# Banded attention and a mixture layer in one kernel: another order for the first fourteen steps

## The chip, the cores and the metric

The kernel runs on one core of a Trainium2 chip. The metric is the device time of one execution in microseconds (us). The engines are PE (matrix products), DVE (element-wise and reductions), ACT (activations, copies), POOL (another element-wise engine) and SP, which here only issues loads and stores.

## The reference

```python
k_sum = k.reshape(B, H, nb, block, D).max(axis=3)
v_sum = v.reshape(B, H, nb, block, D).mean(axis=3)
mask_l = np.abs(pos[:, None] - pos[None, :]) < window
scores_s = scale * np.einsum('bhsd,bhnd->bhsn', q, k_sum) + np.log(block)
scores_all = np.concatenate([np.where(mask_l, scores_l, -1e9), scores_s], axis=-1)
a = softmax(scores_all)          # over window keys and block keys together
x = (a @ np.concatenate([v, v_sum], axis=2)) as tokens x 512
h = x @ w_in
P = a[0] + a[1] * h + a[2] * h**2 + a[3] * h**3
Q = 1.0 + np.abs(b[0]) * np.abs(h) + np.abs(b[1]) * h**2
out = (P / (Q + 1e-06)) @ w_out
```

(shortened; the lines of the softmax are drawn together.) There are B = 4 images, H = 8 heads, S = 768 positions, D = 64, block 32 and window 16; 3072 tokens go through w_in (512 x 2048) and w_out (2048 x 512).

## The kernel before

**Tiles.** A *half* is 64 query positions of all eight heads: 12 per image, 48 in all. A half needs 96 window keys and the 24 block keys, so its scores are a 128 x 480 tile. Eight halves are the 512 tokens of one *group*, of which there are six. The 2048 hidden units are cut into 16 *chunks* of 128. A *step* is one group with one chunk: 12 matmuls of layer 1 (`moe1`), the rational activation (the "gelu" of the names), 12 matmuls of layer 2 (`second_layer`).

**A half** (`half`) goes: scores on PE (`sc`), mask and minimum on DVE (`ss`, `sm`), exponentials and sums on ACT, reciprocal of the sum on DVE, normalization on POOL or DVE, transpose on PE (`pt`), copy of it on DVE or ACT (`pts`), product with the value rows on PE (`av`), then the sum as a rounded part `xh` (ACT or DVE) and a rest `xl` (DVE). The first eight halves are the inputs of group 0; halves 8 to 15 follow between the steps.

**The value rows** of a half are 96 loaded rows (`vw0`, `vw1`, `vr0` to `vr3` and two in `vlast`) and, below them, the 24 block means. These means are made once for image 0 by 10 products on PE (`vf`), copied twice by ACT (into `vw0` and `vw1`) and from there six times by POOL (`first_means`).

**The weights** of a chunk come in one load of 1 MB (`w_load`, tile `wr`) as 64-bit numbers and are turned on the chip into a high part and a low part: ACT scales the upper words (`Prelu`), POOL takes a byte of the lower words, DVE shifts and joins the two, ACT rounds the high part into `wearly`, and DVE subtracts for the low part (`w_split`, one token for each). There are four buffers for these loads; a chunk's buffer comes free when its low part is done.

**The order.** Up to step 13 a string, `TEXT`, says in what order all this is issued. Each token is a letter and a number: `K` and `k` load and reduce the keys of image 0 (`I` and `i` of image 1), `Q` loads queries, `V` value rows of a half, `A` windows of later halves, `F` and `G` value tiles, `S` sets constants, `W` loads a weight chunk, `w` does the next part of its split, `h` the next part of a half, `v` a product for the value means, `m` the copies of the means, `x` a third of layer 1 of a step, `ga` to `gk` a part of its activation, `y` a quarter of layer 2, `u` and `n` the means of image 1. The class `Kept` chains the instructions of each engine, and SP's loads, in the order of the text:

```python
if self.last is not None:
    tc.add_manual_dep(ins, self.last, ORDERED, reason="order of the text")
if self in strict:
    self.last = ins.name
```

So within an engine nothing passes anything else; between engines only semaphores count. Behind the text a loop runs over the remaining steps, with only PE in a fixed order.

Of the kernel before, what the change touches and what calls it, by code (L numbers as in the profile page):

```python
# [44 lines left out]
LAG = 3  # L45
SOFF = 12
NWARM = 6
TEXT = ("K2 K1 K0 Q0 K3 Q1 k2 k0 V2 V0 F0 V5 V1 k1 S0 k3 h0 h1 W0 V6 h0 V4 V3 h0 h1 h0 V7 W1 A8 h1 A9 h2 h3 h0 h2 h4 h3 v2 h1 h2 h3 h2 h4 v9 h0 h0 v0 h3 h1 h6 h2 v1 w0 h3 h2 W2 h3 "
# [11 lines left out]
AVGW = NK + NB - 4  # L60
AVGH = NK + NB - 2
NREST = (S - HPG * HQ) // P
# [22 lines left out]
def tile_kernel(ctx, tc, qw_in, kraw, kwin, vpad, vred, wio, a, b, cmask, cident, cavg, out):  # L85
# [635 lines left out]
    strict |= {pe, dve, act, gps, syn}  # L721
    for what in TEXT.split():
        token(what.rstrip("0123456789"), int(what.lstrip("abcdefghijklmnopqrstuvwxyzABCDEFGHIJKLMNOPQRSTUVWXYZ")))
# [99 lines left out]
```

## Time and profile before

| | |
|---|---|
| median of 3 runs | 637.9 us (636.54 to 637.99) |
| span of the profiled execution | 636.9 us |
| PE busy in that span | 620.4 us, 97% |
| DVE busy | 568.5 us, 89% |
| ACT busy | 457.1 us, 72% |
| POOL busy | 256.9 us, 40% |

The page gives no other time of the profiled execution than its span, the time from its first to its last instruction. Busy shares are means over the whole span; the text covers only the first 146 us or so, and there the engines stand in another relation to each other.

### The profile page before, as it was taken

The page shows a single profiled execution, that of the slowest core. Times are in us where ns is not written, and L with a number is a line of the kernel's source. Part 1 is how long each engine was busy: PE and PEld are TensorE (multiplying, and loading weights), DVE is VectorE, ACT ScalarE, POOL GpSimd, SP SyncE. Part 2 cuts the span into 40 slices and gives each one's busy share as a digit, 9 for nine tenths or more (in the row PEclk, how much of TensorE's full clock was granted, in tenths as well). Part 3 has the DMA queues.
Part 4 walks back from the last instruction along what each step waited for, and adds up shares of the span by engine and source line. Part 5 has one row for each costly group of instructions (what it writes and reads, how often), then busy time and mean ns, then how long its engine had stood idle before and what let it go on. Part 6 is the DMA issues. An engine that isn't in the chain of part 4 may idle for free.

```text
span 636.9 us, 11880 instructions
## 1 busy us (share of the span) xinstructions
PE 620.4 (97%) x4078; PEld 494.2 (78%) x4078; DVE 568.5 (89%) x1155; ACT 457.1 (72%) x1020; POOL 256.9 (40%) x344
## 2 busy tenths in 40 slices
PE   8899999999999999999999999999999999999997
PEld 4466777778788878888888777888888888888886
DVE  5799999999898999889988989988988989898885
ACT  3789999877867757767767768667777765656662
POOL 1366679654434336233143244243234242222221
PEclk9999999999999999999999999999999999999999
DMA  9977777413434434324423433323333120100001
GB/s 289 341 281 233 242 220 232 165 40 126 148 113 136 138 114 155 106 99 138 134 89 120 136 124 101 95 72 106 93 132 100 57 65 1 63 4 1 1 2 66
DMA packets 51752, 77.66 MB, mean 122 GB/s; under 512 B 6260, under 2 KB 33524, under 8 KB 49772
## 3 DMA queue, kind: packets, MB, share of 16 engines
q1 hardware_dynamic: 50412, 74.75, 36.2%
q0 software_dynamic: 560, 1.77, 1.4%
q8 instruction: 32, 0.52, 0.3%
q10 hardware_dynamic: 720, 0.38, 0.2%
q14 instruction: 28, 0.23, 0.1%
HBM read 60.33 MB, written 14.73 MB: 118 GB/s over the span
## 4 chain that ended last, share of the span: by engine, by line
PE 62%; DVE 21%; ACT 6%; DMA 5%; issue 3%; POOL 2%; DVEq 0%; POOLq 0%; ACTq 0%
PE po L113 29%; PE h L113 28%; DVE tu L113 6%; DVE tq L113 5%; PE av L113 3%; DVE gh L113 2%; PE sc L113 2%; DMA wr<-in_wio_dram 2%; DVE wr L113 2%; ACT ta L113 2%; DMA kres<-in_kraw_dram 1%; DVE ss L113 1%; POOL ss L113 1%; DMA w<-wr 1%; ACT ss L113 1%
## 5 line engine op out<-in xcount | busy, mean ns | idle before, releaser
L113 POOL TENSOR_TENSOR gl<-tu,ta 128x512 fp32r<-128x512 f32 x96 | 129.4, 1348 | 296.5 <-DVE tu L113 140.3
L113 ACT ACTIVATE ta<-tq,cs 128x512 f32<-128x512 f32 x96 | 69.8, 727 | 80.5 <-DVE tq L113 79.6
L113 PE MATMUL po<-wearly,gh 128*128 128x512 f32 x384 | 120.3, 394 | 0.7 <-ACT o L113 0.7
L113 PE MATMUL po<-w,gh 128*128 128x512 f32 x384 | 119.7, 393 | 0.0
L113 POOL TENSOR_SCALAR ss<-ss,sm 128x120 f32<-128x120 f32 x176 | 84.3, 497 | 41.6 <-DVE sm L113 40.7
L113 PE MATMUL h<-xh,wearly 128*128 128x512 f32 x384 | 97.8, 394 | 1.6 <-DVE tu L113 1.0
L113 PE MATMUL h<-xh,w 128*128 128x512 f32 x384 | 96.8, 391 | 1.4 <-DVE sm L113 0.9
L113 PEld LDWEIGHTS h<-xh,wearly 128*128 128x128 f32 x384 | 71.5, 188 | 18.2 <-ACT ta L113 1.0
L113 PEld LDWEIGHTS po<-wearly,gh 128*128 128x128 f32 x384 | 70.8, 188 | 18.0 <-ACT o L113 2.4
L113 PEld LDWEIGHTS h<-xh,w 128*128 128x128 f32 x384 | 71.5, 188 | 17.0 <-ACT ta L113 1.3
L113 DVE SCALAR_TENSOR_TENSOR gh<-tu,cs,ta 128x512 fp32r<-128x512 f32 x96 | 73.8, 768 | 10.9 <-ACT ta L113 1.4
L113 PEld LDWEIGHTS po<-w,gh 128*128 128x128 f32 x384 | 71.2, 188 | 15.7 <-issue 1.1
L113 ACT ACTIVATE ss<-ss,sm 128x120 f32<-128x120 f32 x188 | 71.7, 385 | 12.2 <-DVE sm L113 12.2
L113 ACT ACTIVATE tu<-h,cs 128x512 f32<-128x512 f32 x96 | 74.7, 778 | 0.5 <-PE h L113 0.5
L113 PE MATMUL po<-w,gl 128*128 128x512 f32 x192 | 74.9, 390 | 0.0
L113 PE MATMUL po<-wearly,gl 128*128 128x512 f32 x192 | 74.8, 390 | 0.0
L113 DVE SCALAR_TENSOR_TENSOR tu<-tu,cs,tq 128x512 f32<-128x512 f32 x96 | 72.2, 753 | 2.6
L113 DVE SCALAR_TENSOR_TENSOR tu<-tu,cs,h 128x512 f32<-128x512 f32 x96 | 71.1, 741 | 2.2
L113 DVE SCALAR_TENSOR_TENSOR tq<-tq,gh 128x512 f32<-128x512 f32 x96 | 66.6, 694 | 2.7
L113 ACT ACTIVATE ta<-h,cs 128x512 f32<-128x512 f32 x95 | 64.6, 680 | 4.8 <-POOL gl L113 4.8
L113 DVE TENSOR_TENSOR tu<-tu,h 128x512 f32<-128x512 f32 x96 | 64.9, 676 | 0.1
L113 ACT ACTIVATE ta<-ta 128x512 f32<-128x512 f32 x96 | 60.8, 633 | 2.7
(92 smaller groups left out, 917.3 us busy)
## 6 DMA issues: line engine op xcount, KB each, us to landing
wr<-in_wio_dram SPq DMA_DIRECT2D x15, 1024.0 KB
cross<-tb SPq DMA_DIRECT2D x32, 256.0 KB
vw<-in_vpad_dram SPq DMA_DIRECT2D x42, 192.0 KB
kw<-in_kwin_dram SPq DMA_DIRECT2D x40, 192.0 KB
pts<-cross SPq DMA_DIRECT2D x96, 64.0 KB
out_dram<-o SPq DMA_DIRECT2D x23, 256.0 KB
qw<-in_qw_dram SPq DMA_DIRECT2D x40, 128.0 KB
kr<-in_kraw_dram SPq DMA_DIRECT2D x12, 384.0 KB
```

The costliest lines, as they stand in the source:

```text
L113: out = getattr(self.engine, name)(*args, **kw)
```

## The change

Only `TEXT` is replaced. Both lists have the same 566 tokens, and so the same instructions; the first line of each:

```diff
-TEXT = ("K2 K1 K0 Q0 K3 Q1 k2 k0 V2 V0 F0 V5 V1 k1 S0 k3 h0 h1 W0 V6 h0 V4 V3 h0 h1 h0 V7 W1 A8 h1 A9 h2 h3 h0 h2 h4 h3 v2 h1 h2 h3 h2 h4 v9 h0 h0 v0 h3 h1 h6 h2 v1 w0 h3 h2 W2 h3 "
...
+TEXT = ("K2 K0 k0 k2 K1 k1 K3 k3 h8 Q0 h0 Q1 S0 h0 h2 V2 h14 h0 h0 h4 F0 v2 h3 h11 h1 h1 h1 h6 v8 h3 h3 h3 h0 W0 h0 h1 h5 h5 h3 h3 h3 V3 h1 h1 v9 h1 h2 h6 V0 v0 V4 v4 h7 h7 h2 h5 h5 "
...
```

In the words of the kernel: the load of chunk 0 (`W0`) stands behind one half's value rows and ahead of the seven others, where it stood behind four; the scaling of chunk 0 (the first `w0`) stands behind the exponentials of six halves, where it stood behind those of four; the halves come in another order; and more of the splits of chunks 2, 3 and 4 stand ahead of the third part of layer 1 of step 0.

**SP, the first loads.** Here are SP's loads from the first value rows on, in the kernel before (`vr`, `vw` and `vlast` are value rows, `vf0` the value tile, `wr0` chunk 0; `in_cavg` are constants for the means). Ahead of them stand four loads of keys and two of queries in both kernels.

```order
L113 DMA vr0_115<-in_vpad_dram 96x512
L113 DMA vw0_103<-in_vpad_dram 96x512
L113 DMA kres_107<-in_cavg_dram 128x282
L113 DMA vf0_0_141<-in_vpad_dram 128x2x512
L113 DMA vr3_118<-in_vpad_dram 96x512
L113 DMA vw1_104<-in_vpad_dram 96x512
L113 DMA wr0_188<-in_wio_dram 128x2048
L113 DMA vlast_119<-in_vpad_dram 96x512
L113 DMA vr2_117<-in_vpad_dram 96x512
L113 DMA vr1_116<-in_vpad_dram 96x512
```

And after:

```order
L113 DMA vr0_115<-in_vpad_dram 96x512
L113 DMA kres_107<-in_cavg_dram 128x282
L113 DMA vf0_0_264<-in_vpad_dram 128x2x512
L113 DMA wr0_322<-in_wio_dram 128x2048
L113 DMA vr1_116<-in_vpad_dram 96x512
L113 DMA vw0_103<-in_vpad_dram 96x512
L113 DMA vr2_117<-in_vpad_dram 96x512
L113 DMA vlast_119<-in_vpad_dram 96x512
L113 DMA vw1_104<-in_vpad_dram 96x512
L113 DMA vr3_118<-in_vpad_dram 96x512
L113 DMA vlast_119<-in_vpad_dram 96x512
```

With the six loads ahead of these rows, chunk 0 was the thirteenth load and is the tenth; seven value-row loads now stand behind it, where four did.

**ACT, the scaling of chunk 0.** The rows of ACT around that scaling, `ACTIVATE wr0`, before; `ACTIVATE ss` x4 are the exponentials of a half, `ACTIVATE sm` finishes its sums:

```order
L113 ACTIVATE ss2_253,sm2_254<-ss2_253,sm2_254 128x120 x4
L113 ACTIVATE sm2_254<-sm2_254 128x4
L113 ACTIVATE ss3_293,sm3_294<-ss3_293,sm3_294 128x120 x4
L113 ACTIVATE sm3_294<-sm3_294 128x4
L113 ACTIVATE wr0_188<-wr0_188 128x1024
L113 ACTIVATE ss4_307,sm4_308<-ss4_307,sm4_308 128x120 x4
L113 ACTIVATE sm4_308<-sm4_308 128x4
L113 ACTIVATE ss5_383,sm5_384<-ss5_383,sm5_384 128x120 x4
L113 ACTIVATE sm5_384<-sm5_384 128x4
```

And after:

```order
L113 ACTIVATE ss5_329,sm5_330<-ss5_329,sm5_330 128x120 x4
L113 ACTIVATE sm5_330<-sm5_330 128x4
L113 ACTIVATE ss2_356,sm2_357<-ss2_356,sm2_357 128x120 x4
L113 ACTIVATE sm2_357<-sm2_357 128x4
L113 ACTIVATE ss7_372,sm7_373<-ss7_372,sm7_373 128x120 x4
L113 ACTIVATE sm7_373<-sm7_373 128x4
L113 ACTIVATE wr0_322<-wr0_322 128x1024
L113 ACTIVATE ss6_362,sm6_363<-ss6_362,sm6_363 128x120 x4
L113 ACTIVATE sm6_363<-sm6_363 128x4
L113 CAST wearly_105<-wr0_322 128x1024
```

The scaling moved from behind half 3 to behind half 7, the sixth half in the new order (0, 3, 1, 5, 2, 7).

**DVE, around the last inputs of group 0.** The rows of DVE where the last halves' `xl` is made, before; `SCALAR_TENSOR_TENSOR wr` is the shift of a chunk, `TENSOR_TENSOR wearly` the subtraction for its low part:

```order
L113 COPY pts7_574<-pt7_556 120x512
L113 TENSOR_TENSOR xl0_438<-av4_561,xh0_437 128x4x64
L113 SCALAR_TENSOR_TENSOR wr1_211<-wr1_211 128x1024
L113 TENSOR_TENSOR xl0_438<-av7_577,xh0_437 128x4x64
L113 TENSOR_TENSOR xl0_438<-av6_587,xh0_437 128x4x64
L113 COPY kw0_99<-ks0_131 128x96
L113 COPY kw1_100<-ks0_131 128x96
L113 TENSOR_TENSOR wearly_105<-wr1_211,wearly_105 128x1024
L113 SCALAR_TENSOR_TENSOR wr2_371<-wr2_371 128x1024
L113 SCALAR_TENSOR_TENSOR wr3_375<-wr3_375 128x1024
```

And after:

```order
L113 TENSOR_TENSOR xl0_485<-av2_560,xh0_484 128x4x64
L113 TENSOR_TENSOR xl0_485<-av7_571,xh0_484 128x4x64
L113 SCALAR_TENSOR_TENSOR wr3_532<-wr3_532 128x1024
L113 SCALAR_TENSOR_TENSOR wr2_552<-wr2_552 128x1024
L113 TENSOR_TENSOR xl0_485<-av6_586,xh0_484 128x4x64
L113 TENSOR_TENSOR xl0_485<-av4_599,xh0_484 128x4x64
L113 TENSOR_TENSOR wearly_105<-wr3_532,wearly_105 128x1024
L113 SCALAR_TENSOR_TENSOR wr4_556<-wr4_556 128x1024
```

The shifts of chunks 3 and 2 moved ahead of the last two halves' `xl`, and the subtraction of chunk 3 and the shift of chunk 4 now stand right behind them, where the subtraction of chunk 1 and the shifts of chunks 2 and 3 stood.

## Rows read from the trace of the kernel before

**Rows 1.** The core's span and its mean granted clock of TensorE, as a share of full speed.

```profile
core 0: 636.9 us, clock 0.999
```

**Rows 2.** Busy time by stretch of the span: from and to in us, length, then busy us and number of instructions of PE, PE's weight loads, DVE, ACT and POOL, the granted clock, the DMA engines' busy share and GB/s. The last two rows overlap the others.

```profile
0.00:11.40 11.40, 9.78 (x84) 4.66 (x88) 4.45 (x8) 1.28 (x1) 0.20 (x4) 1.00 0.88 282
11.40:25.60 14.20, 12.81 (x214) 7.13 (x207) 9.06 (x67) 8.83 (x39) 4.85 (x10) 1.00 1.05 300
25.60:47.90 22.30, 19.71 (x223) 14.26 (x222) 21.48 (x51) 20.39 (x50) 14.16 (x19) 1.00 0.82 315
47.90:145.30 97.40, 93.27 (x604) 71.13 (x603) 96.16 (x199) 89.34 (x189) 66.30 (x62) 1.00 0.61 190
...
240.00:636.90 396.90, 392.05 (x2343) 321.12 (x2342) 349.85 (x663) 268.48 (x587) 133.15 (x191) 1.00 0.26 82
0.00:20.00 20.00, 17.81 (x279) 10.12 (x280) 11.44 (x59) 7.15 (x29) 2.56 (x9) 1.00 0.95 294
20.00:40.00 20.00, 16.59 (x177) 10.70 (x176) 15.87 (x50) 16.10 (x51) 14.00 (x22) 1.00 0.96 341
```

**Rows 3.** DVE's waits from 0 to 145.3 us: what it was about to do, what it waited for, us in all, times, longest.

```profile
DVE ks L113 <- DMA kres<-in_kraw_dram: 5.6, 3, 3.2
DVE sm L113 <- ACT sm L113: 4.9, 3, 3.5
```

**Rows 4.** The chain of waits that ended last, in order of time: start, us, what.

```profile
10.06 12.52 DMA wr<-in_wio_dram
22.61 1.12 ACT wr L113
...
25.59 1.22 DVE wr L113
```

**Rows 5.** Timeline of ACT: start, us, engine, line, operation, out<-in, shapes, count and, in brackets, the idle time before and what ended it.

```profile
14.24 0.60 ACT L113 ACTIVATE ss<-ss 128x480 f32<-128x480 f32 x1 [0.63 <-POOL ss L113]
...
18.13 0.20 ACT L113 ACTIVATE sm<-sm 128x4 f32<-128x4 f32 x1
22.61 1.12 ACT L113 ACTIVATE wr<-wr 128x1024 f32<-128x1024 f32 x1 [4.27 <-DMA wr<-in_wio_dram]
23.62 0.39 ACT L113 ACTIVATE ss<-ss,sm 128x120 f32<-128x120 f32 x1
...
25.38 0.38 ACT L113 ACTIVATE ss<-ss,sm 128x120 f32<-128x120 f32 x1
...
27.25 1.06 ACT L113 COPY vw<-vf 24x512 f32<-24x512 f32 x2
```

**Rows 6.** Timeline of DVE, the same columns.

```profile
11.43 0.28 DVE L113 CUSTOM_DVE_ANT_0 ss<-sc,mask 128x120 f32<-128x120 f32 x1 [0.40 <-PE sc L113]
...
15.61 0.28 DVE L113 CUSTOM_DVE_ANT_0 ss<-sc,mask 128x120 f32<-128x120 f32 x1 [0.19 <-POOL ss L113]
...
18.37 0.18 DVE L113 RECIPROCAL sm<-sm 128x4 f32<-128x4 f32 x1 [0.81 <-ACT sm L113]
...
21.28 0.69 DVE L113 COPY pts<-pt 120x512 f32<-120x512 f32 x1
25.50 0.18 DVE L113 RECIPROCAL sm<-sm 128x4 f32<-128x4 f32 x1 [3.53 <-ACT sm L113]
25.59 1.22 DVE L113 SCALAR_TENSOR_TENSOR wr<-wr 128x1024 int32<-128x1024 int32 x1
...
30.09 1.30 DVE L113 TENSOR_TENSOR wearly<-wr,wearly 128x1024 fp32r<-128x1024 f32 x1
...
47.14 0.75 DVE L113 SCALAR_TENSOR_TENSOR gh<-tu,cs,ta 128x512 fp32r<-128x512 f32 x1 [0.17 <-ACT ta L113]
...
145.25 0.68 DVE L113 TENSOR_TENSOR w<-wr,w 128x512 fp32r<-128x512 f32 x1
```

**Rows 7.** Timeline of SP's queue: when each load was issued.

```profile
7.43 0.64 SPq L113 DMA_DIRECT2D vf<-in_vpad_dram  x1
...
10.06 0.35 SPq L113 DMA_DIRECT2D wr<-in_wio_dram  x1
...
17.11 0.33 SPq L113 DMA_DIRECT2D kw<-in_kwin_dram  x1
22.60 0.33 SPq L113 DMA_DIRECT2D qw<-in_qw_dram  x1
```

**Rows 8.** DVE's groups of one shape from 0 to 145.3 us: count, busy us, mean ns of one, idle time before them.

```profile
L113 DVE SCALAR_TENSOR_TENSOR wr<-wr 128x1024 int32<-128x1024 int32 x15 | 18.7, 1250 | 0.3 <-issue 0.2
L113 DVE CUSTOM_DVE_ANT_0 ss<-sc,mask 128x120 f32<-128x120 f32 x72 | 15.7, 276 | 0.6 <-PE sc L113 0.4 <-POOL ss L113 0.2
...
L113 DVE TENSOR_TENSOR wearly<-wr,wearly 128x1024 fp32r<-128x1024 f32 x6 | 8.5, 1412 | 0.0
...
L113 DVE TENSOR_REDUCE ks<-kr 128x24 f32<-128x768 f32 x4 | 3.7, 936 | 0.0
...
L113 DVE COPY kw<-ks 128x96 f32<-128x96 f32 x3 | 0.9, 349 | 0.0
```

**Rows 9.** Timeline of POOL, the columns of rows 5.

```profile
14.18 1.39 POOL L113 TENSOR_SCALAR ss<-ss,sm 128x120 f32<-128x120 f32 x4
...
27.97 2.35 POOL L113 COPY vr<-vw 24x512 f32<-24x512 f32 x4 [2.73 <-ACT vw L113]
30.26 2.17 POOL L113 COPY vlast<-vw 24x512 f32<-24x512 f32 x2
...
60.46 4.90 POOL L113 TENSOR_SCALAR ss<-ss,sm 128x120 f32<-128x120 f32 x4
```

22 rows, old and new, of the table TEXT are left out of this document.

## The prediction, made before the changed kernel was run

> **What bounds the kernel now.** First the span and the clock [rows 1]: the profiled execution took 636.9 us, 1.0 us under the median of 637.9, at a granted clock of 0.999, so no term of the sum is a clock term. Then the stages [rows 2]. Behind 240 us PE is busy 392.05 of 396.90 us, and the program there is the same in both kernels: a gain must be earned earlier and is then carried through. From 47.90 to 145.30, where DVE starts its last instruction of the order list, DVE is busy 96.16 of 97.40 us and ACT 89.34: DVE bounds the list. So I count DVE's idle time, span minus busy, in its four stages: 6.95, 5.14, 0.82 and 1.24 us, together 14.15. The list's instructions are the same in both kernels, so DVE's work of 131.15 us stays, and what changes is this idle time.
>
> The waits say what it is [rows 3]: 5.6 us for key loads, 4.9 us in reciprocals for ACT's sums, 3.5 us of it in one piece. The chain of waits gives the place [rows 4]: the load of the first weight chunk, 12.52 us from 10.06, then its scaling on ACT, exponentials, and DVE's shift. In ACT's timeline [rows 5] half 3's sums end at 18.3; then ACT waits 4.27 us for chunk 0 until 22.61, and only then does half 4's exponentials. DVE [rows 6], done with a copy at 21.97, waits 3.53 us until 25.50 for half 4's sums. The chunk landed by 22.6: each load waits for the landing of one some places ahead, and behind its issue at 17.11 SP issues nothing until 22.60 [rows 7].
>
> **The change, part by part.** *Up to the first mask.* The four key loads now go out in a row, and two copies of key maxima into later tiles (349 ns mean [rows 8], some 0.5 us together) stand ahead of the first mask. I put that mask at 11.75 instead of 11.43 with 0.5 us more work done, so idle 6.8 instead of 6.95: a gain of 0.15; the bounds are nothing and 0.5.
>
> *Chunk 0 ahead of the value rows.* Its load is SP's tenth instead of its thirteenth; before's tenth left at 7.43 [rows 7], so it leaves near 7.5 instead of 10.06. Up to and with it 4.85 MB are asked for; with 0.6 to 1.1 MB behind it sharing the engines, at the 0.294 MB/us of the first 20 us [rows 2], it lands at 18.5 to 20.3. ACT reaches it later than that. A half's exponentials take 1.76 us (23.62 to 25.38 [rows 5]), half 1 in one piece 0.60; from 12.07 (11.75 and one mask) five halves and half 1 take 5 x 1.76 + 0.60 = 9.4, to 21.5, and waits for masks in between add 0.5 to 1.6: scaling starts at 22.0 to 23.1. So it does not start earlier than the 22.61 of before; but six halves instead of four are done by then, and ACT's 4.27 us of waiting are filled.
>
> *What waits instead.* DVE's shift of chunk 0 stands behind that scaling, which ends at 23.1 to 24.2 (1.12 us); I have DVE there 0.8 us earlier. Five small waits come in, of kinds that DVE has in before at 0.19 to 0.81 us [rows 6]: masks 4 and 5 behind their scores (0.3), the reciprocals of halves 3 and 2 (0.28, 0.25), the copies of turned halves 0 and 2, whose transposes stand behind value products on PE (0.3, 0.5). With the 0.8 that is 2.4, against 5.14. If each of the five were 0.81, it would be 4.9 and the gain gone; if only the 0.8 stayed, the gain would be 4.3. I take 2.5: the idle time is then 9.3 us where before had 12.1.
>
> *Value rows later.* Seven value-row loads stand behind 1.05 MB more, 3.6 us at 0.294 MB/us, and chunk 1 lands at 27 to 29 (7.6 MB asked for up to it). ACT scales chunk 1 ahead of the value means, which come at about 31 instead of 27.25 [rows 5]. This costs nothing while DVE has masks, turned halves and chunk 0's subtraction ahead of it, until 30.5 by the sum of their durations; were that cover gone, DVE would wait up to 3.6 us for the first attention product.
>
> *More weights ahead of layer 1.* Around the last inputs of group 0 DVE now has the shifts of chunks 3, 2 and 4 and the subtraction of chunk 3; the order pieces show it. By the end of the first gelu product at 47.89 [rows 6] DVE will have done some 3.8 us more than in before: a key reduction, half 9's masks, two shifts, and one subtraction for another [rows 8]. This work is only done earlier, but it needs the loads. Chunk 3's subtraction stands behind ACT's scaling of chunk 4, so chunk 4 must land by 38.7. Up to it 11.1 MB are asked for (keys 1.6, queries 1.05, value rows and tiles 2.1, five chunks 5.2, the rest 1.1), and some 0.8 MB behind it share the engines. 5.88 MB are in by 20 us; the other 6.0 take 17.7 us at 0.341 MB/us and 20.5 at 0.294 [rows 2]: landing at 37.6 to 40.4. That is a wait of 0 to 1.6, and with 0.1 for the rest the idle time at the gelu product is 9.4 to 11.0, against 6.95 + 5.14 + 0.82 = 12.9. The lead there is 1.9 to 3.5; I take 2.8, nearer to the 0.341, which is the rate of these very 20 us.
>
> *The rest of the list.* DVE's idle 1.24 there cannot shrink much. Three things can make it grow. ACT, 92% busy there, comes closer: adding up both engines' durations along the list, I estimate it 0.2 to 0.7 us ahead of DVE's need at three gelu steps, where before had 1 to 3. PE does the last parts of step 4's second layer behind step 5's, so the gelu buffer that step 8 needs comes free, by the same sums, 1.3 us ahead of its use. Chunk 6 lands at about 55, and ACT reaches it at 55.7 to 57. From below this costs nothing, from above three waits near the 0.81 of the small ones, some 2.0. I take 0.5, since each has a margin left. Sum: 2.8 - 0.5 = 2.3 us off; 637.9 - 2.3 = **635.6 us** (the profiled execution: 636.9 to 634.6).
>
> **The rivals.** *B, the lead is spent again.* The list ends as before, because DVE idles some 2 us more from 48 to 145, or because POOL is late: its last two copies of value means take 1.09 us each at 30.26, the four ahead of them 0.59 [rows 9], and DVE's subtraction of 1.30 us started at 30.09 [rows 6]. In the new list a second DVE weight step (1.22 us) can fall beside those copies and hold back the attention products behind them by as much. For it: the thin margins, and 4.90 us for POOL's four normalizing steps at 60.46 that took 1.39 at 14.18 [rows 9]. Against it: that has to fall together with two of the margins before the lead is gone. Time 636.0 to 639.8, middle 638.0.
>
> The Trainium skill, page "SBUF — State Buffer", section "SBUF: two separate sides", says that a VectorE operation with two on-chip inputs and a GpSimd operation that reads on-chip memory take a shared port pair exclusively, so that the later one waits for the whole of the other. By that rule this part of B would happen whenever the two meet, and 635.6 would become 636.8; the trace agrees at 30.26 and 60.46, and shows no place for the copies of the new list.
>
> *C, slower: the weights come late.* Layer 1 of step 0 needs only chunk 0, but the list now has chunks 3, 2 and 4 on ACT and DVE ahead of the last inputs' parts and of the first gelu, and these engines can't pass them. Each us that chunk 4 lands past 38.7 is a us of DVE. It decides at 43.4, where 4.7 us of wait make up the lead of 2.8 and the 1.9 us that can be measured: the 6.0 MB would then move at 0.257 MB/us. For it: the rate varies by stage, 0.282 in the first and 0.190 in the last of the list [rows 2]. Against it: the low one is where few loads are asked for. Time 639.8 to 643.0, at 0.257 to 0.226 MB/us.
>
> *D, larger gain.* Most of the waits that I put into the second and third stage (2.5 and 0.9) aren't there: of 5.14 + 0.82 = 5.96 nearly all would go, 632.0 to 634.4.
>
> *The change does nothing here, since chunk 0's scaling starts no earlier,* is the low end of the forecast: ACT and DVE then only change what they do ahead of it.
>
> **How the numbers follow.** The forecast, 0.5 to 3.5 us off (634.4 to 637.4): 0.50, of which 0.38 lie over 0.3% (1.9 us, about what a measurement of this kernel can tell from no change), below 636.0. B: 0.22, of which 0.08 reach above 639.8 with all margins missed and the rest is within. C: 0.20, of which 0.02 within. D: 0.08, all faster. Faster 0.38 + 0.08 = 0.46; same 0.12 + 0.14 + 0.02 = 0.28; slower 0.08 + 0.18 = 0.26. The range takes D's low end and C's high end, 632.0 to 643.0; the forecast's own is 634.4 to 637.4.
>
> **What would show it.** ACT's scaling of chunk 0 starts at 22 to 23.1 without a wait for its load, which lands by 20.3. DVE's longest wait for ACT's sums is under 1 us, its idle time between 11.4 and 25.6 near 2.5. The first value-mean copy is at about 31. Chunk 4 lands by 40.4 and DVE's subtraction of chunk 3 waits under 1.6. DVE's list ends at 143.6 instead of 145.93 [rows 6], with the same distance from there to the end. I am wrong if DVE waits for weights around 40 us, if POOL's six value-mean copies take over 6 us instead of 4.5, or if DVE idles over 3 us between 48 and the list's end.

## The result, and the profile after

The changed kernel takes 641.75 us (median of 4 runs, 641.09 to 642.53), against 637.22 (636.54 to 637.99) for the kernel before, run beside it: a ratio of 1.0067, 95% interval 1.005 to 1.0084. It is 4.5 us slower, where 2.3 us faster was forecast.

In every run of this study the time is the span plus 1.7 to 1.9 us. The profile before, with its span of 636.9 [rows 1], was thus of a longer execution than most: 56 later runs of the same kernel, beside the experiments below, have spans of 635.1 to 637.6, median 636.0, and four of them are as long. So the two profiles differ by 2.9 us, and the comparison of traces can explain 2.9 of the 4.5 us.

First the stages of the kernel after, in the columns and the stretches of [rows 2], and two us of the second stage:

```profile
core 0: 639.8 us, clock 0.997
```

```profile
0.00:11.40 11.40, 8.61 (x80) 4.18 (x83) 4.60 (x10) 1.28 (x1) 0.20 (x4) 1.00 0.86 279
11.40:25.60 14.20, 12.22 (x224) 7.66 (x217) 10.66 (x69) 11.29 (x52) 5.91 (x12) 0.88 1.04 326
25.60:47.90 22.30, 18.60 (x215) 13.00 (x214) 22.14 (x52) 18.03 (x36) 17.42 (x19) 1.00 0.79 300
47.90:145.30 97.40, 92.04 (x599) 70.12 (x599) 96.00 (x177) 87.28 (x182) 57.79 (x62) 1.00 0.57 183
...
20.00:22.00 2.00, 2.00 (x7) 1.22 (x6) 0.56 (x5) 0.23 (x1) 0.46 (x1) 0.50 1.11 286
```

DVE's idle time is 11.40 - 4.60 = 6.80, then 3.54, 0.16 and 1.40 us, together 11.90, against 14.15 before. The forecast was 6.8, 2.5, 0.8 (by its lead of 2.8) and 1.24 + 0.5, together 11.8. So DVE waits 2.25 us less up to 145.3, as forecast, and yet all that follows comes later.

What grew is the time that the instructions themselves take. One tile's instructions (`gh`, the gelu product) in the kernel before and in the kernel after, each with count, shortest/median/longest in ns:

```profile
L113 DVE SCALAR_TENSOR_TENSOR gh<-tu,cs,ta x14: 715/760/1005, 47.1 to 141.8; 128x512 fp32r<-128x512 f32 x14
L113 DVE SCALAR_TENSOR_TENSOR tq<-tq,gh x14: 675/684/866, 48.6 to 144.6; 128x512 f32<-128x512 f32 x14
```

```profile
L113 DVE SCALAR_TENSOR_TENSOR gh<-tu,cs,ta x14: 723/750/1704, 50.2 to 143.7; 128x512 fp32r<-128x512 f32 x14
L113 DVE SCALAR_TENSOR_TENSOR tq<-tq,gh x14: 676/684/1596, 52.0 to 145.0; 128x512 f32<-128x512 f32 x14
```

The medians are the same within 10 ns; the longest took 1.70 instead of 1.01 us, and 1.60 instead of 0.87. The timelines of DVE and POOL of the kernel after show where:

```profile
57.38 1.60 DVE L113 SCALAR_TENSOR_TENSOR gh<-tu,cs,ta 128x512 fp32r<-128x512 f32 x1
...
71.74 2.10 DVE L113 SCALAR_TENSOR_TENSOR wr<-wr 128x1024 int32<-128x1024 int32 x1
...
97.46 1.60 DVE L113 SCALAR_TENSOR_TENSOR tq<-tq,gh 128x512 f32<-128x512 f32 x1
...
103.77 1.58 DVE L113 SCALAR_TENSOR_TENSOR gh<-tu,cs,ta 128x512 fp32r<-128x512 f32 x1
105.39 0.69 DVE L113 SCALAR_TENSOR_TENSOR tq<-tq,gh 128x512 f32<-128x512 f32 x1
...
126.17 0.68 DVE L113 TENSOR_TENSOR tu<-tu,h 128x512 f32<-128x512 f32 x1
...
126.88 0.75 DVE L113 SCALAR_TENSOR_TENSOR tu<-tu,cs,h 128x512 f32<-128x512 f32 x1
127.76 1.70 DVE L113 SCALAR_TENSOR_TENSOR gh<-tu,cs,ta 128x512 fp32r<-128x512 f32 x1
```

```profile
57.15 1.28 POOL L113 TENSOR_SCALAR wr<-wr 128x1024 int32<-128x1024 uint8 x1 [0.77 <-DMA wr<-in_wio_dram]
...
70.83 1.96 POOL L113 TENSOR_SCALAR wr<-wr 128x1024 int32<-128x1024 uint8 x1
...
97.08 1.43 POOL L113 TENSOR_SCALAR wr<-wr 128x1024 int32<-128x1024 uint8 x1
...
102.86 1.96 POOL L113 TENSOR_SCALAR wr<-wr 128x1024 int32<-128x1024 uint8 x1
...
126.43 1.29 POOL L113 TENSOR_TENSOR gl<-tu,ta 128x512 fp32r<-128x512 f32 x1 [1.50 <-DVE tu L113]
127.81 1.11 POOL L113 TENSOR_SCALAR wr<-wr 128x1024 int32<-128x1024 uint8 x1
```

Each long gelu instruction ends 0.55 us behind the end of a byte step of POOL (the step of the weight split that takes a byte), the shift 1.05: 127.81 + 1.11 = 128.92, and the `gh` that should take 0.75 ends at 129.46. That is most of its own time: the DVE instruction stands still while POOL's step runs, and does so too where its record begins 0.05 us ahead of POOL's, as here. The two instructions with `h` as an input, at 126.17 and 126.88, run beside POOL's `gl` (a product with two inputs) for their usual 0.68 and 0.75: their `h` lies in PE's accumulators, not in the memory that POOL reads. The Trainium skill, page "SBUF — State Buffer", section "SBUF: two separate sides", has the rule for it: a VectorE operation with two inputs in that memory and a GpSimd operation that reads it take a shared port pair exclusively, so whichever is first blocks the other fully. The trace agrees: 0.83 to 0.95 us more for each that meets a byte step from its beginning, and none for those with an input elsewhere.

To count it, I took for each form of DVE instruction the duration that a fifth of them stay under, and added up what single instructions took beyond that, where it is more than 0.15 us ("stretch"), by the POOL instruction that lay beside it longest. Up to the first DVE instruction from which the rest of the program is the same in all kernels (some 206 us):

| kernel (one profile each) | reaches it at, us | DVE idle, us | stretch beside byte steps, us | stretch in all, us |
|---|---|---|---|---|
| before | 206.54 | 19.82 | 3.20 | 4.72 |
| after | 209.25 | 17.95 | 6.95 | 9.49 |

The sum explains the difference: 1.87 us less idle time, 4.77 us more stretch, 2.90 more, and 2.71 is the difference of the times (2.9 at the end). Without any count: DVE's busy time up to that point, time less idle time, is 186.72 us before and 191.30 after, 4.58 more for the same instructions. Of the 4.77, byte steps make 3.75; most of the rest lies beside POOL's `gl` products.

### The profile page after: what moved, and what is told of

Read it like the earlier page. It is cut to its first block, busy times and chain, and to the rows that moved or that the text cites. A ratio compares the mean times of both kernels' runs of the same rounds, so it can differ in the third digit from the quotient of the medians.

```text
span 639.8 us, 11864 instructions
## 1 busy us (share of the span) xinstructions
PE 619.2 (97%) x4078; PEld 494.4 (77%) x4078; DVE 573.6 (90%) x1155; ACT 457.0 (71%) x1020; POOL 252.9 (40%) x344
## 4 chain that ended last, share of the span: by engine, by line
PE 47%; DVE 26%; ACT 11%; issue 5%; POOL 2%; DMA 1%; DVEq 0%; SPq 0%; ACTq 0%; POOLq 0%
PE po L113 23%; PE h L113 21%; DVE tu L113 8%; DVE tq L113 7%; DVE gh L113 4%; ACT ta L113 3%; ACT ss L113 3%; DVE ss L113 2%; PE av L113 1%; POOL ss L113 1%; PE sc L113 1%; DVE wr L113 1%; ACT tu L113 1%; DVE ks L113 1%; DVE tb L113 1%
## 5 line engine op out<-in xcount | busy, mean ns | idle before, releaser
L113 POOL TENSOR_TENSOR gl<-tu,ta 128x512 fp32r<-128x512 f32 x96 | 132.0, 1375 | 304.5 <-DVE tu L113 144.4
L113 POOL TENSOR_SCALAR ss<-ss,sm 128x120 f32<-128x120 f32 x176 | 77.2, 457 | 45.0 <-DVE sm L113 44.2
L113 DVE SCALAR_TENSOR_TENSOR gh<-tu,cs,ta 128x512 fp32r<-128x512 f32 x96 | 77.4, 806 | 11.4 <-ACT ta L113 2.2
```

What stands on the lines that cost most here:

```text
L113: out = getattr(self.engine, name)(*args, **kw)
```

## The experiments

Two theories went in. **P**: POOL's byte steps hold DVE up, and the new order lets more of them meet a DVE instruction that can be held up. **C**: PE falls to half its clock in the new first part (0.50, the lower of its two levels, from 20 to 22 us, above) and what waits for it is the loss. Rows of C, from PE's and ACT's timelines of the kernel after:

```profile
17.74 0.18 PE L113 MATMUL sc<-ks,qres 64*64 64x24 f32 x1 [1.50 <-issue]
...
18.76 1.70 PE L113 MATMUL vf<-vf,kres 128*120 128x512 f32 x2
...
27.01 1.02 PE L113 MATMUL vf<-vw,kres 96*120 96x512 f32 x2
```

```profile
23.53 1.14 ACT L113 ACTIVATE wr<-wr 128x1024 f32<-128x1024 f32 x1
...
31.02 1.06 ACT L113 COPY vw<-vf 24x512 f32<-24x512 f32 x2 [0.75 <-PE vf L113]
```

PE stands 1.5 us without a reason that the profile shows, and behind it a pair of products takes 1.70, where a pair of nearly the same shape takes 1.02 at the full clock. The table speaks against C from the start: what waits for PE would be idle time of DVE, and that is less than before.

**The two halves of the list exchanged.**

```diff
-TEXT = (the old list)
+TEXT = (the new list up to the first x0, then the other tokens in the old order)
```

> The new list up to the first third of layer 1 of step 0 (155 tokens, about 41 us), then the tokens that are left in the order of the old list. Theory P (POOL's byte steps hold DVE up: the DVE instructions that lie beside such a step last longer, 6.95 us in all in the new list against 3.2 in the old one, 1.9 against 0.7 of it in this first part): DVE's idle time stays near 11.9, the stretching falls back to about 4.4, so about 1 us faster than the kernel before, 636.2. Theory C (the loss is in the first part, by PE's fall to half its clock at 18 to 22.7 us and the waits behind it): the whole loss is in this kernel too, 641.7.

Measured 639.24 us, ratio 1.0031 (1.002 to 1.0043). The other way round:

```diff
-TEXT = (the old list)
+TEXT = (the old list up to the first x0, then the other tokens in the new order)
```

> The old list up to the first third of layer 1 (134 tokens), then what is left in the order of the new list. Theory P: DVE's idle time as in the kernel before, stretching in the later part as in the new list (6.3 against 2.9 us), so 3.4 us slower than before, 640.6. Theory C: as the kernel before, 637.2.

Measured 646.19 us, ratio 1.014 (1.0126 to 1.0154). Neither theory hit either number. The stretch is where P puts it (4.99 us in the first, 8.96 in the second, by the same count). Four of the six runs of the first have a full clock, and its profile shows 1.00 throughout the first 40 us: C's fall did not come there, though the first part is the new list's, so this run hardly tests C. And joining two lists at a point makes waits of its own: DVE's idle time is 19.96 and 23.47 us. In the second, DVE waits for a key load that this list asks for right ahead of its use; its waits from 25 to 48 us:

```profile
DVE ks L113 <- DMA kr<-in_kraw_dram: 2.2, 1, 2.2
```

So a mixed list says where the stretch comes from (the later part), and nothing on the sum.

**Both lists without POOL's byte step.**

```diff
-            gps.tensor_scalar(l32, byte, 1.0 / 32, -15.5 / 32, op0=ALU.mult, op1=ALU.add)
...
-                                     op0=ALU.logical_shift_left, op1=ALU.bitwise_or)
+                                     op0=ALU.logical_shift_left, op1=ALU.bitwise_and)
```

> The new list without POOL's byte step of the weight split, as the run before this one. Theory P: 6.95 us of stretching go away, about 634.8, and the distance between the two lists falls from 4.5 to about 0.7 us. Theory C: the distance stays at 4.5 us, 641.7 or 3 to 4 us over the run before this one.

The low parts are then other numbers, but the instructions of DVE are of the same shapes. Measured 635.5 us, ratio 0.9971 (0.9959 to 0.9982) to the kernel before: 6.25 us less than the new list with the step. In the profiles the common point comes 5.13 us earlier (204.12): no stretch beside byte steps is left, 3.40 lie beside `gl` products, and DVE idles 18.80 us. The instruction that took 1.60 at 57.38 is back at its usual time; DVE's timeline of this kernel:

```profile
55.84 0.75 DVE L113 SCALAR_TENSOR_TENSOR gh<-tu,cs,ta 128x512 fp32r<-128x512 f32 x1
```

> The old list without POOL's byte step of the weight split (the lower words are used as they are, so the low parts are other numbers). Theory P: the 3.2 us by which DVE's instructions beside these steps are longer go away: about 634. Theory C: nothing changes, 637.2.

Measured 638.48 us, ratio 1.0019 (1.0009 to 1.0029): slower by 1.1, where 3 us faster was expected. The byte steps' stretch is gone, but POOL then reaches its `gl` products at other times, and these hold DVE up for 3.44 us instead of 1.11; and DVE's idle time is 20.78 instead of 19.82. So a stretch taken away is not a gain by itself. Without byte steps the new list is 3.0 us faster than the old one, where with them it is slower by 4.5 us (by 3.25 in the last round, below): which list is faster turns on these steps, as P says and C does not. (P had 0.7 us slower for the new list, and did not see the reversal.) PE kept its full clock in this profile of the new list, so the profile alone does not part the two theories; but two of its six runs have 0.996 and 0.997, the clock of the runs with byte steps, and take 635.7 and 635.24 us.

**The kernel before once more**, unchanged, for a second profile.

> The kernel before, unchanged, for a second profile of it: its runs lie between 636.5 and 638.8 us, and the profile that the prediction was read from has a span of 636.9 where these runs have 635.1 to 637.0. Expected: a span near 635.5, and the same stretched DVE instructions beside POOL's byte steps, 3 to 4 us up to 146 us, in both theories; if the stretching varies by a us or more between two profiles of one kernel, then sums over single profiles carry that much doubt.

Measured 637.69 us, ratio 0.9993 (0.9983 to 1.0003); a span of 636.6, idle time 19.16, stretch 5.44 (3.94 beside byte steps). Single profiles of one kernel thus differ by 0.7 us in either sum. For the stretch one meeting is enough: the same shift and the same byte step, first in the profile before, then in this one:

```profile
55.39 1.22 DVE L113 SCALAR_TENSOR_TENSOR wr<-wr 128x1024 int32<-128x1024 int32 x1
55.39 2.22 POOL L113 TENSOR_SCALAR wr<-wr 128x1024 int32<-128x1024 uint8 x1
```

```profile
54.80 2.17 DVE L113 SCALAR_TENSOR_TENSOR wr<-wr 128x1024 int32<-128x1024 int32 x1
54.78 1.11 POOL L113 TENSOR_SCALAR wr<-wr 128x1024 int32<-128x1024 uint8 x1
```

The same two instructions meet, and once POOL is held up by a us, once DVE. A few hundredths of a us decide which, so a list's stretch is in part chance.

**The byte step in pieces.**

```diff
-            gps.tensor_scalar(l32, byte, 1.0 / 32, -15.5 / 32, op0=ALU.mult, op1=ALU.add)
+            for c in range(4):
+                part = slice(c * DM // 4, (c + 1) * DM // 4)
+                gps.tensor_scalar(l32[:, :, part], byte[:, :, part], 1.0 / 32, -15.5 / 32, op0=ALU.mult, op1=ALU.add)
```

(with 2 for 4 in the halves.)

> The new list, with POOL's byte step cut into four instructions of a quarter each. Theory P: DVE's instructions then wait for a piece of 0.3 to 0.5 us instead of a step of 1.1, so of the 6.95 us of stretching about 3 are left: 637 to 638.5. Theory C (and any in which POOL's work itself, not the length of one instruction, is what costs): no faster than 641.7, rather slower, as POOL has more to do.

> The old list with the same cut. Theory P: of 3.2 us of stretching some 1.5 are left, so 1 to 2 us faster, 635.5 to 636.5. Theory C: no change, 637.3, or slower.

> The new list with POOL's byte step in two instructions of half the size (0.65 us each by the row of the last chunk, against 1.1 to 1.3). Theory P: a DVE instruction is held up by at most half as much, so 3 to 4 of the 7 us are left, while POOL has only 0.2 us more for each chunk and does not come late as with the quarters: 638.5 to 640. If cutting it costs as much as it saves, as with the quarters, 641.5.

> The old list with the same cut. Theory P: of 3 to 4 us of stretching about half is left, 1 to 1.5 us faster, 636.3. If POOL comes late as with the quarters (DVE waited 3.9 us for byte steps there): 639 to 641.

Measured: the new list 641.51 with quarters (ratio 1.005, 1.0037 to 1.0063) and 640.83 with halves (1.0049, 1.0036 to 1.0062); the old one 644.79 (1.0112, 1.0097 to 1.0127) and 638.56 (1.0012, 1.0004 to 1.0021). In the new list the size of the piece sets the stretch, as P says: beside byte steps 6.95, 4.83 and 1.69 us for one, two and four pieces. In the old list quarters lower it to 1.2 us, while halves leave it at 3.2, as in its first profile. In the new list the same `gh` takes 0.90 beside quarters:

```profile
60.47 0.90 DVE L113 SCALAR_TENSOR_TENSOR gh<-tu,cs,ta 128x512 fp32r<-128x512 f32 x1
```

The time did not follow: all four runs are slower than P had them, and only the new list gains, by less than a us. Three quarter steps take 1.89 us where a whole one takes 1.28, POOL comes late, and DVE now waits for it; DVE's waits of the new list with quarters, and after that the quarters themselves in POOL's timeline:

```profile
DVE wr L113 <- POOL wr L113: 2.8, 3, 1.8
```

```profile
60.25 1.89 POOL L113 TENSOR_SCALAR wr<-wr 128x256 int32<-128x256 uint8 x3 [0.78 <-DMA wr<-in_wio_dram]
```

**Chunk 0 alone.** The old list, with the load and the first three parts of the split of chunk 0 moved (and the value tile's load `F0` one place, ahead of `V0`).

```diff
-V2 V0 F0 V5 V1 k1 ... W0 V6 ...
+V2 F0 W0 V0 V5 V1 k1 ... V6 ...
...
-v1 w0 h3 h2 ... G0 h0 w0 h4 h4 w0 h4 v8 v6 v4 h5 h5 v3
+v1 h3 h2 ... G0 h0 h4 h4 h4 v8 v6 v4 h5 h5 w0 w0 w0 v3
```

> The old list with nothing moved but chunk 0: its load ahead of seven value-row loads (behind that of half 2), and its scaling, byte step and shift behind the exponentials of halves 4 and 5. By the prediction's working this takes the 3.5 us wait out of DVE's list and puts about 0.8 in its place: 2 to 2.7 us faster, 634.7 to 635.3, if nothing else moves. If the byte steps fall otherwise (theory P), the time differs by up to 1.1 us for each DVE instruction that then stands beside one.

Measured 641.1 us, ratio 1.0049 (1.003 to 1.0069), with an unusual spread: 638.3 to 640.1 in six runs with a clock of 0.997 to 1.0, and 642.1 to 644.6 in six with 0.991 to 0.995. The profile is of the fastest run. There the wait of 3.53 us for half 4's sums is gone, and what the prediction put in its place is there at about its size:

```profile
24.96 1.23 DVE L113 SCALAR_TENSOR_TENSOR wr<-wr 128x1024 int32<-128x1024 int32 x1 [1.03 <-ACT wr L113]
```

But the other small waits came too, and DVE's idle time up to the common point is 18.95 us, 0.2 less than in the second profile of the kernel before and 0.9 less than in the first, not 2 to 2.7 less. And half of the runs, with a lower clock, are 2 to 6 us longer than the others. What makes the clock fall in them, and whether the fall or what led to it costs the time, was not seen, as no profile is of one of them.

**The new list again, and with two more products of zeros at the start.**

> The new list unchanged, for more runs and a second profile. Its runs so far all have a granted clock of 0.997. Theory P: about 641.7 whatever the clock of a run, and again some 7 us of stretched DVE instructions beside byte steps. Theory C: runs with a clock of 0.999 to 1.0 are 1.5 us or more faster than those with 0.997, and lie near 640.

Measured 641.09 us, ratio 1.0062 (1.005 to 1.0074), clocks 0.995 and 0.997; beside it the kernel before took 637.84, so the loss is 3.25 us here. In its profile PE has its full clock from 18 to 24 us and falls later, the value means come at 29.83 instead of 31.02, and yet the time is 642.43: the stretch is 10.46 us.

```diff
-NWARM = 6
+NWARM = 8
```

> The new list with eight instead of six products of zeros at PE's start. They fill some 1.0 us of the 1.33 us that PE waits ahead of its first scores at 10.2, so that PE goes into the stall at 16.2 us with less idle time behind it. Theory P: nothing changes, 641.7, or up to 0.5 slower if the scores come later. Theory C: the clock stays at 1.0 from 18 to 23 us, the value means on ACT come at 30 instead of 31, and the time falls by 1 to 1.5 us to about 640.3.

Measured 641.4 us, ratio 1.0066 (1.0048 to 1.0085): four runs with a clock of 1.0 at 640.7 to 641.8, two with 0.995 at 642.3 and 645.0. At 20 to 22 us, where the new list had 0.50:

```profile
20.00:22.00 2.00, 2.00 (x12) 1.21 (x11) 1.41 (x11) 1.12 (x6) 0.54 (x1) 1.00 1.07 264
```

At a full clock the new list, with a median of 640.95 us in those four runs, is still 3.1 us over the 637.84 of the kernel before beside it, and 0.1 us under the same list at 0.995 and 0.997 in the same round. In the profiles DVE's idle time up to the common point is 17.05 us at the full clock and 17.95 in the kernel after. So C is worth 0.1 to 0.9 us by these runs (why the two runs at 0.995 take 1.4 and 4.0 us more than that median stays open); what turns the gain into a loss is P.

## Why the prediction was wrong

**What bounds the kernel.** Right: the common point moves with DVE's time, idle plus busy, and what is won or lost there arrives at the end (2.71 us there, 2.9 at the end); in all fourteen profiles the end follows 430.0 to 430.8 us behind that point.

**The idle time.** Right in sum, 11.90 against 11.8, in part by luck: the second stage had 1.0 us more than forecast, the third and fourth 1.0 less. Up to the common point DVE idles 1.87 us less than in the first profile of the kernel before, 1.21 less than in the second, against a forecast of 2.3. Chunk 0's scaling started at 23.53 without a wait for its load, where 22.0 to 23.1 was forecast; POOL's byte step, which waits only for the load, began at 19.35, inside the 18.5 to 20.3 for the landing; the value means came at 31.02 (about 31), which is luck too, as they come at 29.83 where PE keeps its clock. The second stage idled 3.54 instead of 2.5: half 7's mask, not on my list of small waits, waited 1.72 for transposes that PE's stall and half clock had made late. Where PE had its full clock there, in the new list again and with two more products, the stage idles 2.35 and 2.64:

```profile
11.40:25.60 14.20, 12.25 (x220) 7.81 (x213) 11.85 (x78) 12.45 (x57) 7.13 (x14) 1.00 1.05 330
11.40:25.60 14.20, 12.48 (x251) 8.25 (x241) 11.56 (x74) 12.14 (x57) 6.81 (x13) 1.00 1.05 323
```

The third idled 0.16.

**The step that failed** is a sentence of the first part: that DVE's work of 131.15 us stays because the instructions are the same. Their durations depend on what POOL does beside them. Up to the common point the same instructions keep DVE busy 4.58 us longer: before, 4.72 us of DVE's work were time lost beside POOL; after, 9.49. Nothing in the sum had a place for that. The signs were there: in [rows 8] the mean of the subtraction is 1412 ns, where a single one in [rows 6] takes 1.30 us, and in [rows 9] four steps of POOL take 4.90 us that took 1.39 earlier.

**Rival B** had the right pair of engines and the wrong one as the victim: it priced POOL's copies waiting for DVE (they took 3.28 + 2.17 us, 0.9 more, and cost nothing that the trace shows) and not DVE waiting for POOL. The rule that it quotes makes the later one wait, whichever it is; I used one direction. Its margins of ACT and PE held: DVE's idle time from 47.9 to 145.3 is 1.40.

**Rival C**, late weights (not the theory C above), gave a range that holds the time that came, by luck, for it did not happen. DVE's waits of the kernel after up to 150 us have no weight load in them:

```profile
DVE ks L113 <- DMA kres<-in_kraw_dram: 4.5, 1, 4.5
DVE ss L113 <- PE sc L113: 2.7, 3, 1.5
DVE ss L113 <- POOL wr L113: 1.7, 1, 1.7
...
DVE wr L113 <- issue: 0.3, 1, 0.3
```

(The third row is that mask. POOL's step had ended a us before it began; what ended just then, at 21.31, are PE's transposes of half 3, whose buffer half 7 takes.) The forecast of 0.26 for slower stood on this wrong mechanism for the most part.

**The announced signs** of being wrong (waits for weights, slow copies, over 3 us of idle time in the list) all stayed away: waits alone could not show the loss. Of the signs of being right, the list's end failed. It was to come at 143.6; DVE's last low part is done at 146.26, and two masks of later halves that stood ahead of it before come behind it:

```profile
145.58 0.68 DVE L113 TENSOR_TENSOR w<-wr,w 128x512 fp32r<-128x512 f32 x1
```

**What stays open**: the 1.6 us between the 2.9 of the profiles and the 4.5 of the medians, part of which is that the profile before is of a longer run, and part that the four runs beside it were short (637.22, where three later rounds have 637.39, 637.88 and 637.84); why the old list without byte steps idles 1 us more; and why some runs of one kernel have a lower clock.

## What to carry to other kernels

When an order changes on an engine that is 99% busy, as DVE is from 47.9 to 145.3 us, its work is not a constant: look at shortest, median and longest duration of each of its instruction forms before adding up waits, and price what the new order puts beside them. A POOL instruction of 1.1 us can cost DVE 0.9 us each time it meets an instruction with two inputs in their common memory, or be held up itself; cutting it into pieces shrinks each hit and can cost as much in POOL's own time. A wait that is filled gives only what no smaller wait takes back: 0.2 to 0.9 us here, where 2 to 2.7 was expected.

## What the runs showed of the hardware

PE's stall at 17.74 was in each of the seven profiles whose first part is the new list's, 1.15 to 1.75 us long, and always behind the same record of PE's stream, the 449th of weight loads, products and sequencer entries; with two more products ahead, which moves all other work eight records down the stream, it stayed behind the 449th. So it belongs to a place in the stream of instructions, not to a piece of work. What PE waits for there no profile shows. In the old list PE comes to that place some 2 us later and waits there 0.69 us at most (with halves), and in two of seven profiles not at all.
